# An attention and Fourier-mix kernel on one core: more weight decoding and hidden-layer work placed around the second batch's folds

## The chip, the cores and the metric

The kernel runs on one core of a Trainium2 chip. The core has a matrix engine (TensorE, in the profile PE, its weight loads PEld), a vector engine (VectorE, DVE), an activation engine (ScalarE, ACT), a general engine (GpSimd, POOL) and a queue that mostly starts transfers (SyncE, SP). Each engine takes its instructions in the order in which they stand in its program, and waits at an instruction until what that needs is there. The metric is the device time of one execution in microseconds (us).

## The reference

Everything is float32, except that the two weight matrices arrive as 64-bit floats. Four batches of 768 rows go through two blocks. First, causal attention with decay in 8 heads of width 64 (`lam` has one decay per head; it is written as a recurrence over blocks of 64 rows with a state of 64 x 64):

```
kv_state = lam_block * kv_state + (kb * rev_pow)^T vb
out      = ((qb kb^T) * Dmask) vb + (qb * lam_pow) kv_state
```

Its output, heads side by side, is a matrix x of 768 x 512 per batch. Then a Fourier mix and a two-layer network:

```
u   = x + real(fft(fft(x, axis=rows), axis=columns))
un  = (u - mean(u)) / sqrt(var(u) + 1e-6)          # each row
out = u + max(un @ w_ch1, 0) @ w_ch2               # 512 -> 2048 -> 512
```

## The kernel before, in words

**Attention** (`attn`, made of `attn_in` and `attn_out`) takes a batch in 6 chunks of 128 rows and the heads in 4 pairs. `attn_in` loads k, q and v (SP), transposes k and q on TensorE (L274, L279) and copies them (ScalarE L276, L281; VectorE L285 for the decayed q). `attn_out` makes scores (L298), multiplies them with the decay (VectorE L302), updates the state (L315, L320) and makes the transposed output (L328, L332), which ScalarE copies to `oT` (L335). `back` turns that into rows again: a transpose on TensorE (L348) and two copies by ScalarE (L350, L351), the second half of the columns reversed.

**The Fourier mix** (`fft_ln`) needs each row beside its mirror image, row 768 - s, to add and subtract the two ("fold"), which quarters the matrix products. The batches get the mirrored rows in two ways:

- The first batch (it is in `TURNED`) keeps a second, reversed copy of the transposed output, `oTs` (ScalarE L386; L392 in the last chunk), and transposes that too (`mirrored`).
- The others write their rows to DRAM from ScalarE's queue (L358, L360, L362) and read them back in mirrored order with indirect transfers of POOL (`mirror_a`, L431 and L437; `mirror_b`, L444).

VectorE then folds in several steps, `fold_a` over rows and `fold_b` over the rest (`fold_x` L418 to L422; L462 to L476). TensorE does the transform over rows (L508), ScalarE copies it (L512), and for three row tiles in turn TensorE does the one over columns (`width`, L521 to L526); VectorE puts the results together and adds x (L588 to L592, row 384 apart in L598 to L601). `norm` computes statistics (L538, L539, and L542, L543 on POOL), normalises (L556), and transposes on TensorE with a copy by ScalarE (L561, L562), or for groups that are used late writes the transposed rows to DRAM (L570) and u itself (L576).

**The weights** are decoded from 64-bit floats in 32 chunks (`load_weights`). A chunk is one transfer of 512 KB (SP, L209), two ScalarE instructions (L216, a sign; L218) and five on VectorE (L217, L220, L222, L224, L225). The raw chunk uses the same 4 buffers (`hp`) as the hidden layer. The order of the chunks is first half of `w_ch1`, first half of `w_ch2`, then the two second halves; the first 16 are what the first half of the hidden layer needs.

**The network** (`mlp`) takes 2 row tiles (a group) at a time, 12 groups in all. The first four (`PLAIN`) are computed directly: hidden blocks of 128 (L625, 4 products each), rectified in turn by ScalarE and VectorE (`fc % 2`; L633, L631) from a PSUM pool of 3 tiles, then the second product (L639), whose sum is added to u (L646, L647 for a first half; L650, L651 and a store for the rest). Three of the four are split into two halves of the hidden layer, `half[0]` and `half[1]`, so that work can start before all weights are decoded. The other eight groups (`late`) follow with fewer products (L712, L759), after VectorE has made sums of the weights (`combine_weights`, L689) and of their inputs (L702 to L705).

**The order of the work** is written by generators. Each yields an estimate of the time of what it has just issued, and `weave` and `beside` draw on two or more of them so that their estimates run in proportion: a larger yield lets the other generator issue more before the first goes on. A scheduler may then move instructions on an engine, except those pinned by `keep_in_program_order`. The lines around the change, L838 and L839:

```
run(beside(part(mix, T_FOLD), T_FOLD, att1, 2.5 * t_chunk))
run(beside(mix, 24.0, beside(att1, 3.5 * t_chunk, w, 0.12 * NW), 0.12 * NW + 2.5 * t_chunk))
```

Here `mix` is the first batch's Fourier mix, `att1` the second batch's attention, `w` the decoding, `NW` is 32. After that, the rest of the front (`fr`: second batch's last attention and its mix, then batches three and four) is woven with `half[0]` and the decoding, and later with `half[1]` and the fourth plain group. When the front is done, VectorE combines weights while TensorE finishes the plain groups; then comes `late`, from 440 us to the end.

Of the kernel before, what the change touches and what calls it, by code (L numbers as in the profile page):

```python
# [76 lines left out]
def kernel(  # L77
# [10 lines left out]
    nc = tc.nc  # L88
    B, H, S, D = q.shape
    DM = H * D  # L90
    DFF = moe_w_ch1.shape[1]
    C = 128
    NC = S // C
    HC = NC // 2
    HP = H // 2
    NK = S // 4 + 1
    KO = DM // 128
    FO = DFF // 128
# [3 lines left out]
    BLK = [128, S // 4 + 1 - 128]  # L102
# [12 lines left out]
    def front_pool(name, bufs):  # L115
        return front_end.enter_context(tc.tile_pool(name=name, bufs=bufs, side="left"))
# [8 lines left out]
    fp = front_pool("fp", 1)  # L125
# [13 lines left out]
    def new(pool, shape, tag, **kw):  # L139
        cnt[0] += 1  # L140
        return pool.tile(shape, F32, tag=tag, name=f"{tag}{cnt[0]}", **kw)
# [112 lines left out]
    ins, oTs, eo = {}, {}, {}  # L254
    LEADS = (0,)
    TURNED = (0,)
    first = const.tile([128, HP, 1], F32, name="first")
# [31 lines left out]
    def attn_out(b, c, head):  # L289
        kT, qT, qs, kd, vt = ins.pop((b, c))  # L290
        last = c == NC - 1


        mm = nc.tensor.matmul
        pss = [psum_a([C, HP, C]) for _ in range(2)]
        for hp in range(HP):
            for hi in range(2):
                mm(pss[hi][:, hp, :], lhsT=kT[HD[hi], hp, :], rhs=qT[HD[hi], hp, :], start=True, stop=True)  # L298
        sc = []
        for hi in range(2):  # L300
            t = new(at, [C, HP, C], "sc", bufs=3)
            nc.vector.tensor_tensor(t, pss[hi], decay[:, hi::2, :], op=ALU.mult)  # L302
            sc.append(t)
        if last and b - 1 in LEADS:
            mirror_a(b, pin=True)
        yield 1.5


        s_old, s_new = st[(c + 1) % 2], st[c % 2]
        if not last:  # L310
            pu = psum_a([128, HP, D])
            for hp in range(HP):
                for hi in range(2):
                    h = 2 * hp + hi
                    mm(pu[HD[hi], hp, :], lhsT=kd[:, h, :], rhs=vt[:, h, :], start=True, stop=True)  # L315
            if c == 0:
                nc.vector.tensor_copy(s_new, pu)
            else:
                nc.gpsimd.tensor_tensor(s_new, s_old, spow.broadcast_to([128, HP, D]), op=ALU.mult)
                nc.vector.tensor_tensor(s_new, s_new, pu, op=ALU.add)  # L320
            yield 0.9


        po = psum_a([128, HP, C])
        if c > 0:
            for hp in range(HP):
                for hi in range(2):
                    mm(po[HD[hi], hp, :], lhsT=s_old[HD[hi], hp, :], rhs=qs[HD[hi], hp, :],  # L328
                       start=(hp == 0), stop=False, skip_group_check=True)
        for hp in range(HP):  # L330
            for hi in range(2):
                mm(po[HD[hi], hp, :], lhsT=vt[:, 2 * hp + hi, :], rhs=sc[hi][:, hp, :],  # L332
                   start=(c == 0 and hp == 0), stop=(hp == HP - 1), skip_group_check=True)
        oT = new(at, [128, HP, C], "oT")
        nc.scalar.copy(oT, po)  # L335
        if b in TURNED:

            if c == 0:
                nc.scalar.copy(first, po[:, :, 0:1])
            elif c > 1:  # L340
                nc.scalar.copy(oTs[b][:, :, 0:1], po[:, :, 0:1])
        yield 2.0
        yield from head

        def back(oT, x, n=128):
            px = psum_a([C, HP, 128])
            for hp in range(HP):
                nc.tensor.transpose(px[:, hp, :], oT[:, hp, :], ident)  # L348
            px = px.rearrange("p h e -> p (h e)")
            nc.scalar.copy(x[0:n, 0:HM], px[0:n, 0:HM])  # L350
            nc.scalar.copy(x[0:n, HM:DM], px[0:n, DM - 1:HM - 1:-1])  # L351

        if b not in TURNED:
            x = xn_[b, c] = new(xp, [C, DM], "x") if c < HC else new(xn, [C, DM], "xn")
            back(oT, x)
            if c == 0:
                xd[b] = (dram.tile([S - 256, DM], F32, name=f"xa{b}"), dram.tile([257, DM], F32, name=f"xb{b}"))
                nc.scalar.dma_start(xd[b][1][256:257], x[0:1])  # L358
            elif not last:
                nc.scalar.dma_start(xd[b][0][(c - 1) * C:c * C], x)  # L360
            if c >= NC - 2:
                nc.scalar.dma_start(xd[b][1][(c - NC + 2) * C:(c - NC + 3) * C], x)  # L362
            if c == NC - 2 and b - 1 not in LEADS:
                mirror_a(b)
            elif last:
                mirror_b(b)
            yield 1.7
            return


        if c == 2:
            eo[b] = new_eo()

        def mirrored(m):
            if m < HC:
                back(oTs[b], eo[b][HC - 1 - m][1][:, 1, 0:DM], BLK[HC - 1 - m])
            else:
                u = xs[b, HC + NC - 1 - m] = new(xp, [128, DM], "x")
                back(oTs[b], u)

        if c > 1:
            mirrored(c - 1)
            yield 1.4
        if c > 0:
            oTs[b] = new(fp, [128, DM + 4], "ds")[:, 0:DM].rearrange("p (h c) -> p h c", h=HP)
            nc.scalar.copy(oTs[b][:, :, C - 1:0:-1], po[:, :, 1:C])  # L386
        if not last:
            x = xn_[b, c] = new(xp, [C, DM], "x") if c < HC else new(xn, [C, DM], "xn")
            back(oT, x)
            yield 1.7  # L390
        else:
            nc.scalar.copy(oTs[b][:, :, 0:1], first)  # L392
            mirrored(c)
            for t in range(HC):
                xs[b, t] = xn_.pop((b, t))
            yield 1.4
# [86 lines left out]
    def fft_ln(b):  # L483
# [7 lines left out]
        if b in LEADS:  # L491
            yield from fold_a(b)
            yield from fold_b(b, sets)
            yield 2.0
        else:
            yield 1.0
            run(fold_a(b))
            yield 3.0
            run(fold_b(b, sets))
            yield 9.0  # L500


        for i in range(5):
            ps = psum_a([128, 2, NK])
            m = 128 if i < 4 else 1
# [72 lines left out]
        for t in (1, 2, 0):  # L578
# [7 lines left out]
            ds = new(fp, [128, 2 * (HM + 2)], "ds")  # L586
# [3 lines left out]
            u, v_ = xs[b, t], xs[b, HC + t]  # L590
# [27 lines left out]
    def mlp(b, g, f0=0, f1=FO):  # L618

        ut = uts[b, g]  # L620
        hr = []
        for fc in range(f0, f1):
            ps = psum_m([128, G * 128])
            for c in range(KO):
                nc.tensor.matmul(ps, lhsT=w1[:, c, 128 * fc:128 * fc + 128], rhs=ut[:, c, :],  # L625
                                 start=(c == 0), stop=(c == KO - 1))
            if fc % 4 == 0:
                hr.append(new(hp_, [128, 4, G * 128], "hr"))
            t = hr[-1][:, fc % 4, :]
            if fc % 2:  # L630
                nc.vector.tensor_scalar(t, ps, 0.0, None, op0=ALU.max)  # L631
            else:
                nc.scalar.activation(t, ps, AF.Relu)  # L633
            yield 1.7
        for i in range(G):
            T = TT[g][i]
            ps = psum_m([128, DM])
            for fc in range(f0, f1):
                nc.tensor.matmul(ps, lhsT=hr[(fc - f0) // 4][:, fc % 4, 128 * i:128 * i + 128], rhs=w2[:, fc, :],  # L639
                                 start=(fc == f0), stop=(fc == f1 - 1))  # L640
                if fc % 4 == 3 and fc < f1 - 1:
                    yield 3.4
            u = xs[b, T]
            tt = nc.vector.tensor_tensor
            if f1 < FO:
                tt(u[:, 0:HM], ps[:, 0:HM], u[:, 0:HM], op=ALU.add)  # L646
                tt(u[:, HM:DM], ps[:, DM - 1:HM - 1:-1], u[:, HM:DM], op=ALU.add)  # L647
            else:
                y = new(up, [128, DM], "y", bufs=1)
                tt(y[:, 0:HM], ps[:, 0:HM], u[:, 0:HM], op=ALU.add)  # L650
                tt(y[:, HM:DM], ps[:, HM:DM], u[:, DM - 1:HM - 1:-1], op=ALU.add)  # L651
                store(b, T, y)
            yield 3.4
# [156 lines left out]
    def run(gen):  # L810
        return sum(gen)
# [12 lines left out]
    NW = 2 * KO * DFF // WP  # L824
    w = weights()
    t_chunk = 7.3
# [3 lines left out]
    def beside(lead, t, other, t_other):  # L830
        return weave(lead, part(other, t_other), t_other / t)

    att1, mix = attn(1), fft_ln(0)
    att0 = attn(0)
    run(part(att0, 2.7))
    run(beside(att0, NC * t_chunk - 2.7, w, 0.25 * NW))

    run(beside(part(mix, T_FOLD), T_FOLD, att1, 2.5 * t_chunk))  # L838
    run(beside(mix, 24.0, beside(att1, 3.5 * t_chunk, w, 0.12 * NW), 0.12 * NW + 2.5 * t_chunk))  # L839

    half = [[mlp(b, g, h * FO // 2, (h + 1) * FO // 2) for b, g in PLAIN[:3]] for h in range(2)]
    fr = chain([att1, fft_ln(1)] + [front(b) for b in range(2, B)])
# [4 lines left out]
    back = chain(half[1] + [mlp(*PLAIN[3])])  # L847
# [47 lines left out]
```

## Time and profile before

| what | value |
|---|---|
| device time, 6 runs | 828.12, 832.36, 832.6, 832.81, 832.88, 833.83 us; median 832.7 |
| the profiled execution | 833.2 us, of it 831.1 us from the first to the last instruction (the span); granted TensorE clock 0.993 of full |
| busy share of the span | PE 96%, PEld 77%, DVE 53%, ACT 22%, POOL 10% |

An execution's profile records each instruction with its start, its duration and the semaphores that it waited for. A row such as `L631 DVE ... x32 | 13.2, 412 | 32.7 <-PE pm L625 32.6` says: line 631, on VectorE, 32 instructions, 13.2 us busy in all, 412 ns on average; before them VectorE stood 32.7 us, of which 32.6 ended when line 625 of TensorE had written tile `pm`. In a timeline row come the start (us), the duration (us), engine, line, operation, tiles and shapes, and in brackets how long the engine stood before it, and what ended that. An engine name with a q (ACTq) is its instruction queue, where it starts transfers.

TensorE's time that went neither into its records nor their usual spacing lies in the front: PE is busy 55.58 of 62 us from 50 to 112 us, 13.90 of 18 from 112 to 130, 29.24 of 30 from 130 to 160, all of 160 to 260, 56.52 of 60 from 260 to 320, 89.94 of 92 from 320 to 412, and all of 412 to 440. VectorE is busy 52.08 of 62 from 50 to 112, and 25.01 of 28 from 412 to 440.

### The profile page before, as it was taken

The numbers are of one execution on the slowest core, as the hardware profiler recorded it, in microseconds if no ns is written. First come the engines' busy times: TensorE is split into PE (matmuls) and PEld (weight loads), VectorE is DVE, ScalarE is ACT, GpSimd is POOL, SyncE is SP. The second block draws the span as 40 slices with busy tenths as digits, with TensorE's granted clock in tenths as the row PEclk, the third lists the DMA queues.
The fourth block names the chain that finished last, engine by engine and source line by source line (L and its number), as shares of the span: only waits on it lengthen the run. The fifth ranks groups of instructions, "written<-read, shape, count | busy, mean of one in ns | idle before, by whom it ended". The sixth has DMA issues, their size and how long they took to land.

```text
span 831.1 us, 11682 instructions
## 1 busy us (share of the span) xinstructions
PE 799.7 (96%) x4608; PEld 636.4 (77%) x4608; DVE 443.5 (53%) x1030; ACT 183.0 (22%) x436; POOL 79.3 (10%) x102
## 2 busy tenths in 40 slices
PE   6989889999999999999999999999999999999998
PEld 5767765758675857767748888888888888888886
DVE  6889788857943582345895551156312561145411
ACT  4745343125520210312101210022001220012100
POOL 3112140012010110220100000000000000000000
PEclk9999999999999999999999999999999999999999
DMA  9966632247951128430442011100111001100010
GB/s 261 249 141 179 159 115 80 84 122 184 234 153 39 51 55 161 111 120 18 114 108 95 1 51 51 51 1 0 52 51 51 0 1 35 36 32 1 1 39 25
DMA packets 126683, 68.87 MB, mean 83 GB/s; under 512 B 111150, under 2 KB 112174, under 8 KB 126630
## 3 DMA queue, kind: packets, MB, share of 16 engines
q1 hardware_dynamic: 121488, 55.67, 26.3%
q0 software_dynamic: 2112, 6.69, 2.5%
q10 hardware_dynamic: 3030, 5.78, 1.9%
q8 instruction: 36, 0.59, 0.3%
q14 instruction: 17, 0.14, 0.1%
HBM read 48.72 MB, written 19.40 MB: 82 GB/s over the span
## 4 chain that ended last, share of the span: by engine, by line
PE 79%; DVE 11%; issue 4%; DMA 3%; ACT 2%; POOL 1%; POOLq 0%; DVEq 0%; ACTq 0%
PE p L759 23%; PE p L712 23%; PE pm L639 10%; PE pm L625 7%; PE pa L508 3%; PE pa L332 3%; PE pa L298 3%; PE pa L328 2%; DMA x<-xb,ix 2%; PE pa L274 1%; PE pa L315 1%; PE pa L348 1%; DVE stt L538 1%; PE pa L279 1%; DMA xb<-xn 1%
## 5 line engine op out<-in xcount | busy, mean ns | idle before, releaser
L625 PE MATMUL pm<-ut,w 128*128 128x256 f32 x512 | 119.1, 382 | 0.2 <-DVE hr L631 0.2
L639 PE MATMUL pm<-w,hr 128*128 128x512 f32 x256 | 118.0, 605 | 1.3 <-DVE hr L631 1.3
L625 PEld LDWEIGHTS pm<-ut,w 128*128 128x128 f32 x512 | 94.3, 190 | 15.4 <-issue 3.1
L712 PE MATMUL p<-ur,w 128*128 128x256 f32 x384 | 93.8, 379 | 0.0
L639 PEld LDWEIGHTS pm<-w,hr 128*128 128x128 f32 x256 | 46.9, 191 | 51.0 <-issue 47.6
L712 PEld LDWEIGHTS p<-ur,w 128*128 128x128 f32 x384 | 73.0, 190 | 10.3 <-issue 0.5
L712 PE MATMUL p<-us,w1s 128*128 128x256 f32 x256 | 65.7, 379 | 0.0
L759 PE MATMUL p<-w,hs 128*128 128x256 f32 x256 | 58.0, 379 | 0.5 <-DVE y L780 0.5
L759 PE MATMUL p<-w2s,hs 128*128 128x256 f32 x256 | 57.9, 379 | 0.0
L759 PE MATMUL p<-w,ha 128*128 128x256 f32 x256 | 57.9, 379 | 0.0
L759 PEld LDWEIGHTS p<-w,hs 128*128 128x128 f32 x256 | 48.5, 190 | 7.5 <-DVE y L780 0.9
L759 PEld LDWEIGHTS p<-w2s,hs 128*128 128x128 f32 x256 | 48.6, 190 | 6.6
L712 PEld LDWEIGHTS p<-us,w1s 128*128 128x128 f32 x256 | 48.6, 190 | 6.6
L759 PEld LDWEIGHTS p<-w,ha 128*128 128x128 f32 x256 | 48.6, 190 | 6.6
L614 POOL DMA_INDIRECT out_dram<-y,ix x12 | 11.9, 988 | 408.5 <-DVE y L785 344.0
L739 ACT COPY ha<-p 128x256 f32<-128x256 f32 x32 | 11.9, 372 | 169.1 <-PE p L712 139.4
L750 DVE TENSOR_TENSOR ha<-p,ha 128x256 f32<-128x256 f32 x32 | 13.6, 424 | 44.9 <-ACT ha L749 44.9
L302 DVE TENSOR_TENSOR sc<-pa,decay 128x512 f32<-128x512 f32 x48 | 31.3, 681 | 11.6 <-PE pa L298 11.6
L332 PE MATMUL pa<-sc,v 128*64 128x128 f32 x384 | 31.5, 281 | 5.4 <-DVE sc L302 5.4
L298 PEld LDWEIGHTS pa<-qT,kT 64*128 64x128 f32 x384 | 26.4, 195 | 12.1 <-ACT qT L281 5.4
L332 PEld LDWEIGHTS pa<-sc,v 128*64 128x64 f32 x384 | 22.9, 137 | 14.2 <-DVE sc L302 9.2
L298 PE MATMUL pa<-qT,kT 64*128 64x128 f32 x384 | 31.2, 295 | 2.5 <-ACT qT L281 2.2
(144 smaller groups left out, 1135.5 us busy)
## 6 DMA issues: line engine op xcount, KB each, us to landing
raw<-in_moe_w_ch_dram SPq DMA_DIRECT2D x32, 512.0 KB, 4.8
k<-in_k_dram SPq DMA_DIRECT2D x24, 256.0 KB, 4.8
q<-in_q_dram SPq DMA_DIRECT2D x24, 256.0 KB, 5.2
v<-in_v_dram SPq DMA_DIRECT2D x24, 256.0 KB, 3.7
ud<-x SPq DMA_DIRECT2D x16, 256.0 KB, 2.3
utd<-e SPq DMA_DIRECT2D x64, 64.0 KB, 2.2
u<-ud SPq DMA_DIRECT2D x16, 256.0 KB, 2.7
ur<-utd SPq DMA_DIRECT2D x6, 512.0 KB, 4.4
```

Of the source, the lines that this page charges most:

```text
L298: mm(pss[hi][:, hp, :], lhsT=kT[HD[hi], hp, :], rhs=qT[HD[hi], hp, :], start=True, stop=True)
L302: nc.vector.tensor_tensor(t, pss[hi], decay[:, hi::2, :], op=ALU.mult)
L328: mm(po[HD[hi], hp, :], lhsT=s_old[HD[hi], hp, :], rhs=qs[HD[hi], hp, :], start=(hp == 0), stop=False, skip_group_check=True)
L332: mm(po[HD[hi], hp, :], lhsT=vt[:, 2 * hp + hi, :], rhs=sc[hi][:, hp, :], start=(c == 0 and hp == 0), stop=(hp == HP - 1), skip_group_chec ...
L508: mm = nc.tensor.matmul(ps[0:m, n, :], lhsT=piece(a, i, n), rhs=cs[0:rows, a, i in (2, 3), n, :], start=(a == 0), stop=(a == 1))
L614: nc.gpsimd.indirect_dma_start(out=out.rearrange("b s d -> (b s) d"), out_offset=row_of(2 + HC * (b + 1) + T - HC), in_=y[:, :], in_offset ...
L625: nc.tensor.matmul(ps, lhsT=w1[:, c, 128 * fc:128 * fc + 128], rhs=ut[:, c, :], start=(c == 0), stop=(c == KO - 1))
L639: nc.tensor.matmul(ps, lhsT=hr[(fc - f0) // 4][:, fc % 4, 128 * i:128 * i + 128], rhs=w2[:, fc, :], start=(fc == f0), stop=(fc == f1 - 1))
L712: nc.tensor.matmul(ps, lhsT=s2.A[a][:, kt, 128 * i:128 * i + 128], rhs=U[b][:, kt, :], start=(first and kt == 0), stop=(kt == 1), skip_gro ...
L739: nc.scalar.copy(a11, two(X))
L750: V.tensor_tensor(a22, two(Z), a22, op=ADD)
L759: nc.tensor.matmul(ps, lhsT=h[a][:, s, i, :], rhs=s2.B[b][:, i, :], start=(first and i == 0), stop=(i == HF - 1), skip_group_check=True)
```

## The change

Four edits, all to the placement of work; what is computed stays the same.

1. In the first batch's attention, `back` is split into its transposes (`turn`) and its copies (`put`). The transposes of the previous chunk's mirrored rows are issued first, then the copies that fill the next `oTs` (now pinned in program order), then the copies of the mirrored rows.
2. For the second batch (`b - 1 in LEADS`) `fft_ln` yields 6.0 instead of 3.0 after `fold_a`, and 12.0 instead of 9.0 after `fold_b`.
3. In `half[0]` (`f1 < FO`) ScalarE does all rectifications; elsewhere they go on taking turns.
4. Beside the first batch's mix and the second batch's attention, 0.16 of the 32 chunks of weights are drawn instead of 0.12.

The diff:

```diff
@@ attn_out
-        def back(oT, x, n=128):
+        def turn(oT):
             px = psum_a([C, HP, 128])
             for hp in range(HP):
                 nc.tensor.transpose(px[:, hp, :], oT[:, hp, :], ident)
-            px = px.rearrange("p h e -> p (h e)")
+            return px.rearrange("p h e -> p (h e)")
+
+        def put(px, x, n=128):
             nc.scalar.copy(x[0:n, 0:HM], px[0:n, 0:HM])
             nc.scalar.copy(x[0:n, HM:DM], px[0:n, DM - 1:HM - 1:-1])
+
+        def back(oT, x):
+            put(turn(oT), x)
...
-        def mirrored(m):
+        def mirrored(m, px):
             if m < HC:
-                back(oTs[b], eo[b][HC - 1 - m][1][:, 1, 0:DM], BLK[HC - 1 - m])
+                put(px, eo[b][HC - 1 - m][1][:, 1, 0:DM][0:BLK[HC - 1 - m]], BLK[HC - 1 - m])
             else:
                 u = xs[b, HC + NC - 1 - m] = new(xp, [128, DM], "x")
-                back(oTs[b], u)
-
+                put(px, u)
+
+        px = turn(oTs[b]) if c > 1 else None
+        if c > 0:
+
+            oTs[b] = new(fp, [128, DM + 4], "ds")[:, 0:DM].rearrange("p (h c) -> p h c", h=HP)
+            tc.keep_in_program_order(nc.scalar.copy(oTs[b][:, :, C - 1:0:-1], po[:, :, 1:C]))
+        if last:
+            tc.keep_in_program_order(nc.scalar.copy(oTs[b][:, :, 0:1], first))
         if c > 1:
-            mirrored(c - 1)
+            mirrored(c - 1, px)
             yield 1.4
-        if c > 0:
-            oTs[b] = new(fp, [128, DM + 4], "ds")[:, 0:DM].rearrange("p (h c) -> p h c", h=HP)
-            nc.scalar.copy(oTs[b][:, :, C - 1:0:-1], po[:, :, 1:C])
         if not last:
             x = xn_[b, c] = new(xp, [C, DM], "x") if c < HC else new(xn, [C, DM], "xn")
             back(oT, x)
             yield 1.7
         else:
-            nc.scalar.copy(oTs[b][:, :, 0:1], first)
-            mirrored(c)
+            mirrored(c, turn(oTs[b]))
             for t in range(HC):
                 xs[b, t] = xn_.pop((b, t))
             yield 1.4
@@ fft_ln
         else:
             yield 1.0
             run(fold_a(b))
-            yield 3.0
+            yield 6.0 if b - 1 in LEADS else 3.0
             run(fold_b(b, sets))
-            yield 9.0
+            yield 12.0 if b - 1 in LEADS else 9.0
@@ mlp
-            if fc % 2:
+            if fc % 2 and f1 == FO:
                 nc.vector.tensor_scalar(t, ps, 0.0, None, op0=ALU.max)
             else:
                 nc.scalar.activation(t, ps, AF.Relu)
@@ the order
-    run(beside(mix, 24.0, beside(att1, 3.5 * t_chunk, w, 0.12 * NW), 0.12 * NW + 2.5 * t_chunk))
+    run(beside(mix, 24.0, beside(att1, 3.5 * t_chunk, w, 0.16 * NW), 0.16 * NW + 2.5 * t_chunk))
```

## The prediction

> **What bounds the kernel now.** I read the engines' shares first, then the stretches, the waits, and the timeline round the longest wait.
>
> ```profile
> PE 799.7 (96%) x4608; PEld 636.4 (77%) x4608; DVE 443.5 (53%) x1030; ACT 183.0 (22%) x436; POOL 79.3 (10%) x102
> ```
>
> TensorE sets the time. Its 4608 records are the same work after the change, so only time in which it stands, or runs at a lower clock, can be won or lost. By stretches (columns: span; busy us of PE, PEld, DVE, ACT, POOL; granted clock; DMA share, GB/s):
>
> ```profile
> 60.00:80.00 20.00, 16.94 (x174) 13.70 (x170) 19.96 (x42) 9.17 (x19) 4.40 (x5) 1.00 0.78 217
> 120.00:130.00 10.00, 6.88 (x18) 3.36 (x17) 8.09 (x21) 0.48 (x3) 0.78 (x1) 0.84 0.16 52
> 130.00:140.00 10.00, 10.00 (x47) 6.83 (x46) 8.66 (x21) 4.40 (x9) 0.00 (x0) 0.99 0.40 110
> 200.00:260.00 60.00, 60.00 (x417) 42.35 (x416) 38.90 (x79) 23.47 (x47) 8.37 (x8) 1.00 0.64 164
> ```
>
> Up to about 110 us VectorE is the limit (19.96 of 20); from 160 TensorE is full, but for short holes at the later folds. The worst ten microseconds are 120 to 130: PE busy 6.88, clock 0.84. The timeline tells why:
>
> ```profile
> 111.52 0.27 DVE L601 TENSOR_TENSOR x<-pa,xn 1x128 f32<-1x128 f32 x1
> 112.50 0.33 ACTq L362 DMA_DIRECT2D xb<-xn  x1
> 115.48 4.04 POOL L444 DMA_INDIRECT x<-xb,ix  x1 [0.54 <-DMA xb<-xn]
> 121.91 0.69 DVE L418 TENSOR_TENSOR fe<-x,x 128x512 f32<-128x512 f32 x1 [3.02 <-DMA x<-xb,ix]
> 125.38 0.57 PE L508 MATMUL pa<-cs,fe 128*128 128x193 f32 x2 [3.12 <-DVE fe L467]
> ```
>
> The second batch's last attention rows are written to DRAM (112.50), gathered back mirrored (115.48, landing 6.41 later), folded by VectorE (121.91), and only then comes the first length transform, L508. VectorE waited 3.02 for the gather, TensorE 3.12 for VectorE. The two engines that rectify:
>
> ```profile
> L631 DVE TENSOR_SCALAR hr<-pm 128x256 f32<-128x256 f32 x32 | 13.2, 412 | 32.7 <-PE pm L625 32.6
> L633 ACT ACTIVATE hr<-pm 128x256 f32<-128x256 f32 x32 | 12.2, 383 | 72.2 <-PE pm L625 68.7 <-DMA ur<-utd 3.5
> ```
>
> Prices of TensorE work: 32 records of L625 took 7.07 us at 247.74, so a block of 8 (one column block) is 1.77; 32 of L639 took 13.90, so the 16 of a row tile are 6.95.
>
> **The change part by part.** Order below means the order in which the changed kernel's instructions stand on each engine.
>
> *Work behind the second batch's folds* (two yields, 3 more each, and rectification off VectorE). Before, the first L508 stands after the first hidden blocks and one L639. After, between L601 and that L508 stand L332 (1.0), three L625 blocks (5.3), the norm's transposes and the row transposes L348 (0.9 and 0.6), two more blocks (3.5) and both row tiles of L639 (13.9): 25.2 us. Against it runs the chain of the fold, and this gets longer: the row copies (L350) now stand on ScalarE behind both copies of a norm's transposes, so they wait for statistics (1.3), POOL (1.1), the two normalisations among fold steps (about 3) and transposes and copies (1.5): 7 after L601, where they stood at 0.03. Then copies 0.65, xb write 2.7, issue 0.3, gather 6.4: 17.1; then the 8.2 that L418 took to the second L467 (121.91 to 130.1): 25.3 to 25.6. TensorE thus waits about 0.5 instead of 3.12: gain 2.6. Bounds: 3.1 if the gather lands in its median 3.4; below nothing if it lands 5 later.
> With the hole goes the lower clock: 0.84 over 10 us is 1.6 us of clock; taken whole, bounds 0 and 1.6. The Trainium skill, page "TensorE: Matmul & The Clock Gate", section "Why this matters for your kernels", wants no idle gap above about 3 us; the 3.12 ahead of the 0.84 agrees. By it 0.5 us of waiting is harmless and 1.6 comes back; by a stricter reading of the row, nothing does.
>
> *Chunks of weights moved.* One chunk is one 512 KB load on SP, two ScalarE instructions (683, 720 ns) and five on VectorE (L217 450, L222 431, L220 440, L224 709, L225 764, in a row 0.34, 0.34, 0.34, 0.60, 0.60: 2.2 us). The order has five instead of four of them ahead of the first batch's second norm, and two and a half more between the second batch's folds. The latter, 5.4 us, lie in the time in which VectorE would wait for the gather. The former lies on the stage that VectorE bounds: cost up to 2.2. Against it VectorE idled 2.96 at 94 for qT, and the order now puts the width steps L588 ahead of that wait. I take 0.5 lost; bounds 2.2 lost and 1.0 won. The loads pass the ud stores on SP, which wait until the norm anyway (x row tiles freed for batch 2 are asked for some 15 us later); where that cover goes, it is a few us of attention.
>
> *Rectification by ScalarE.* Twelve instructions leave VectorE (0.34 each in a row, 4.0 us) and cost ScalarE 12 by 0.38 (4.6). ScalarE was busy 4.4 of 10 at 130 to 140 and 23.5 of 60 later. The gain is that a hidden block no longer waits behind a fold or a decode on VectorE: at 130 to 160 TensorE lost about 1.9 (28.1 us of work at the paces above in 30). I take 0.7; bounds 1.9, and a loss of 1 if ScalarE is held by a sign step waiting for its load (10.8 in nine waits, the longest 2.9; three hidden tiles in PSUM cover 5 us).
> Here a rule speaks against the change: the Trainium skill, page "ScalarE: Activation LUTs", section "Rules for kernel authors", says relu belongs to VectorE, up to about three times faster in bf16. The rows here have float32 from PSUM: 412 on VectorE, 383 on ScalarE. By the rule's factor the move would cost 12 by 255 ns, 3.1 us of engine time; by the rows it saves 0.03 each. No run here shows bf16.
>
> *First batch's mirrored rows.* TensorE waited 1.32 (50.51) for L392, which stood behind two copies and L386. After, L386 and L392 stand first: L392 can end 0.86 earlier. VectorE idled 0.77 (52.71) just for that chain, so 0.8 is won; bounds 0 and 0.8. In two earlier chunks L386 falls behind a decode step; five PSUM banks cover that.
>
> *The end of the front.* The yields use up six units of the second batch's share, so four more hidden blocks of the last plain group are done before the front ends, and 7.07 us less cover stands after it. Before, L522 ended at 404.9, TensorE went over to L712 at 439.99, and the second operand product, which needs L703, came 1.73 later; L703 ended 436.94: 4.8 us of slack. After, VectorE has two L631 less (0.7): 7.07 - 4.8 - 0.7 = 1.6 lost. Bounds: 0 and 4.
>
> Nothing for the other folds: at the third batch both wait for the mlp's output (L651) as before; at the fourth the first wait (0.92) goes, but the second grows as much, since the fold sets it.
>
> **Sum**, against the profiled execution (831.1 span, 833.2 us): -2.6 -1.6 +0.5 -0.7 -0.8 +1.6 = -3.6, so 829.6. The profiled execution stands 0.5 above the median of the runs, 832.7, so I forecast 829.1.
>
> **Rivals.** About 0.3% (2.5 us) is what a measurement of this kernel can tell from no change.
> A, *more is won*: decode fits into the 2.96 us hole and the end keeps its slack: 829.1 - 0.5 - 1.6 = 827.0. For it: VectorE's idle time before 112. Against: VectorE is full from 412 to 438.
> B, *the hole only moves*: the fold stays 3 us late, the clock falls again, the end costs 1.6: 832.7 - 0.7 - 0.8 + 0.5 + 1.6 = 833.3, no change. For it: the chain starts 7 us later than it did.
> C, *slower*: VectorE runs in order, and ahead of the fold now stands L217 of a chunk whose buffer comes free only about 8.5 after L601. Its load (median 4.8) lands near 13.5, in time for a gather at 17. If write, gather and loads crowd each other so that the fold ends 5 us later, TensorE waits 5.5, the clock falls: 833.3 - 3.1 + 5.5 = 835.7. It decides from about 4.4 us of delay. Against it: the DMA share at 120 to 130 is 0.16.
>
> **How the numbers follow.** Forecast 0.50, A 0.14, B 0.20, C 0.16. Faster holds forecast and A, 0.64; same B, 0.20; slower C, 0.16. The forecast's own range is 826 to 831. The range for 8 in 10 starts at 825.0: with the gains at their upper bounds (3.1, 1.6, 1.9, 0.8, and 1.0 from decode) and the end's 1.6 lost it is 832.7 - 6.8 = 825.9, and about 825 if part of that loss is spared too. It reaches over all of B and up to 835.0, where C begins with 4.4 us of delay (833.3 - 3.1 + 4.9 = 835.1), so that C alone is left out.
>
> **What would show it.** Right: no wait above 1.5 us of L508 for L467 in the second batch, clock 1.00 from 110 on, VectorE at work where it stood 3.02, and TensorE in L639 just ahead of L508. L712 would wait about 1.6 for L703 at the end of the front. Wrong: a new wait of L217 (a decode step ahead of the fold) for its load, L633 waits that hold L625, or L601 more than 2 us later.

## The result, and the profile after

The changed kernel takes 827.45 us (median; 824.87 to 832.5), the kernel before 832.25 us in the same comparison. The ratio is 0.9949, with a 95% interval of 0.9939 to 0.9959: faster by half a per cent, 4.2 us. The profiled execution took 827.11 us, its span is 825.3 instead of 831.1.

The engines' shares on the changed kernel's page:

```profile
PE 794.3 (96%) x4608; PEld 634.3 (77%) x4608; DVE 439.6 (53%) x1018; ACT 186.5 (23%) x448; POOL 76.4 (9%) x102
```

TensorE has the same 4608 records in a shorter span; the twelve rectifications have gone from VectorE's 1030 to ScalarE's 448. The changed kernel's busy times by stretches (columns as in the prediction), three of those shown there and one more:

```profile
60.00:80.00 20.00, 17.15 (x178) 14.19 (x180) 19.97 (x43) 9.56 (x20) 3.83 (x4) 1.00 0.79 220
120.00:130.00 10.00, 10.00 (x30) 5.51 (x29) 6.69 (x14) 3.76 (x7) 2.48 (x2) 1.00 0.73 235
130.00:140.00 10.00, 9.93 (x36) 6.06 (x35) 10.00 (x29) 1.47 (x4) 0.00 (x0) 1.00 0.18 56
430.00:440.00 10.00, 7.66 (x29) 6.21 (x28) 7.15 (x13) 1.49 (x4) 1.08 (x1) 0.83 0.91 291
```

The hole of 120 to 130 us is closed: TensorE is busy 10.00 instead of 6.88, at clock 1.00 instead of 0.84. A new one has opened at 430 to 440: 7.66 busy, clock 0.83. In the kernel before, that stretch reads:

```profile
430.00:440.00 10.00, 10.00 (x25) 4.50 (x24) 8.14 (x10) 0.00 (x0) 0.00 (x0) 1.00 0.80 241
```

The timeline of the changed kernel round the second batch's fold (start, duration, engine, line):

```profile
112.25 0.27 DVE L609 TENSOR_TENSOR x<-pa,xn 1x128 f32<-1x128 f32 x1
...
119.18 0.38 ACT L352 COPY xn<-pa 128x256 f32<-128x256 f32 x1
...
119.86 0.33 ACTq L367 DMA_DIRECT2D xb<-xn  x1
...
122.18 1.54 POOL L452 DMA_INDIRECT x<-xb,ix  x1 [6.53 <-DMA xb<-xn]
...
128.40 0.69 DVE L426 TENSOR_TENSOR fe<-x,x 128x512 f32<-128x512 f32 x1 [2.12 <-DMA x<-xb,ix]
```

and TensorE's part of that timeline:

```profile
132.69 3.60 PE L647 MATMUL pm<-w,hr 128*128 128x512 f32 x8
136.12 3.13 PE L516 MATMUL pa<-cs,fe 128*128 128x193 f32 x16
```

L609 is L601 of before, L352 L350, L426 L418, L516 L508, L647 L639. The chain is longer, as forecast: the row copies start 6.9 us after L609 (forecast: 7), the gather lets VectorE go on 16.1 after (17.1). VectorE still stands 2.12 for it, but TensorE has second products (L647) until the fold is done and goes into L516 with no wait listed.

To see where the rest went I take, for each stretch, its length less TensorE's records at their full spacing in a row (0.216 us for L625 and the late L712 and L759, 0.430 for L639, 0.164 for L508, 0.11 for transposes and L521 to L526, 0.07 for L298, 0.064 for L328 and L332, 0.04 for L315). This is the time that TensorE lost to waits and to a lower clock. "End" runs from the first L712 to the last record.

| lost, us | 0–50 | 50–160 | 160–320 | 320–first L712 | end | sum |
|---|---|---|---|---|---|---|
| before | 19.3 | 22.9 | 10.6 | 4.7 | 0.9 | 58.3 |
| changed | 19.3 | 19.1 | 5.8 | 3.6 | 4.8 | 52.6 |

So 3.8 us were won between 50 and 160, 4.9 from 160 to 320 (mostly the third batch), 1.1 in the fourth batch, and 4.0 were lost at the end: 5.7 of the 5.8 between the spans of these two executions, where the medians differ by less.

### The profile page after: what moved, and what is told of

It reads as the page before. It is cut to its first block, busy times and chain, and to the rows that moved or that the text cites. A ratio compares the mean times of both kernels' runs of the same rounds, so it can differ in the third digit from the quotient of the medians.

```text
span 825.3 us, 11708 instructions
## 1 busy us (share of the span) xinstructions
PE 794.3 (96%) x4608; PEld 634.3 (77%) x4608; DVE 439.6 (53%) x1018; ACT 186.5 (23%) x448; POOL 76.4 (9%) x102
## 4 chain that ended last, share of the span: by engine, by line
PE 77%; DVE 14%; DMA 4%; issue 2%; ACT 1%; POOL 1%; SPq 0%; DVEq 0%; POOLq 0%; ACTq 0%
PE p L767 23%; PE p L720 23%; PE pm L633 9%; PE pm L647 7%; PE pa L516 2%; PE pa L332 2%; PE pa L298 2%; DMA x<-xb,ix 2%; PE pa L328 1%; PE pa L274 1%; DVE sc L302 1%; PE pa L315 1%; PE pa L279 1%; DMA raw<-in_moe_w_ch_dram 1%; DVE stt L546 1%
## 5 line engine op out<-in xcount | busy, mean ns | idle before, releaser
L647 PE MATMUL pm<-w,hr 128*128 128x512 f32 x256 | 116.0, 598 | 0.0
L647 PEld LDWEIGHTS pm<-w,hr 128*128 128x128 f32 x256 | 46.6, 190 | 49.5 <-issue 48.0
L720 PEld LDWEIGHTS p<-ur,w 128*128 128x128 f32 x384 | 73.6, 192 | 10.6 <-issue 0.5
L332 PE MATMUL pa<-sc,v 128*64 128x128 f32 x384 | 31.1, 280 | 8.3 <-DVE sc L302 8.2
L302 DVE TENSOR_TENSOR sc<-pa,decay 128x512 f32<-128x512 f32 x48 | 31.3, 681 | 12.0 <-PE pa L298 12.0
L298 PEld LDWEIGHTS pa<-qT,kT 64*128 64x128 f32 x384 | 25.1, 193 | 12.7 <-ACT qT L281 5.8
L332 PEld LDWEIGHTS pa<-sc,v 128*64 128x64 f32 x384 | 22.7, 137 | 15.3 <-DVE sc L302 10.6
L298 PE MATMUL pa<-qT,kT 64*128 64x128 f32 x384 | 29.8, 292 | 3.4 <-ACT qT L281 3.1
```

Source lines behind the costliest of these rows:

```text
L720: nc.tensor.matmul(ps, lhsT=s2.A[a][:, kt, 128 * i:128 * i + 128], rhs=U[b][:, kt, :], start=(first and kt == 0), stop=(kt == 1), skip_gro ...
```

## The experiments

Each was run beside the kernel before; the ratio is against that. The tables of lost time come from one profiled execution each and carry about 2 us of chance (see the last section); the ratios decide.

### Each part alone

The yields alone:

```diff
-            yield 3.0
+            yield 6.0 if b - 1 in LEADS else 3.0
...
-            yield 9.0
+            yield 12.0 if b - 1 in LEADS else 9.0
```

> Only the two yields of the second batch are raised (6.0 and 12.0); the rest is as before. In the order 10 L639 products of 0.87 us (a pair of records) stand ahead of the second batch's first L508, against 1 before, and one more chunk of decoding between its folds. Theory H (the gain is the hole at the second fold and its lower clock; the loss is cover at the end of the front): the 3.1 us wait of L508 goes and 112 to 130 us loses about 5 us less; L712 then waits for L703 about as long as in the changed kernel (2.3, and a half clock of 3.4 us after it, 1.7): 832.3 - 5.5 + 4 = 831, ratio 0.998. Rival W (the earlier decoding of weights carries the gain, the yields only move work): 832.3, ratio 1.000, or slower by the loss at the end, 1.005.

The weights alone:

```diff
-    run(beside(mix, 24.0, beside(att1, 3.5 * t_chunk, w, 0.12 * NW), 0.12 * NW + 2.5 * t_chunk))
+    run(beside(mix, 24.0, beside(att1, 3.5 * t_chunk, w, 0.16 * NW), 0.16 * NW + 2.5 * t_chunk))
```

> Only the share of weights beside the first batch's mix is raised from 0.12 to 0.16. In the order 7 L639 products stand ahead of the second batch's first L508, against 1, and about two and a half more chunks of decoding between its folds. By the prediction's own sum this part alone costs 0.5 us (ratio 1.001), since the stage up to 112 us is bound by VectorE and the fold is late anyway. Theory W: it carries most of the gain, since 6 more products (5.2 us) fill the hole of 3.1 and the clock stays up, with only one hidden block less of cover at the end: 832.3 - 5 + 1 = 828, ratio 0.995.

ScalarE's rectifications alone:

```diff
-            if fc % 2:
+            if fc % 2 and f1 == FO:
```

> Only the rectifications of the first halves all go to ScalarE. By the prediction's sum: 0.7 us won between 130 and 160 us, ratio 0.999; the order ahead of the second fold is as before, so L508 still waits about 3 us for L467. Rival: the 3.9 us that the changed kernel wins between 260 and 320 us come from here (no hidden tile waiting for L631): 828.4, ratio 0.995.

The mirrored rows alone (the first part of the change, shortened here):

```diff
-        if c > 1:
-            mirrored(c - 1)
+        px = turn(oTs[b]) if c > 1 else None
...
+            tc.keep_in_program_order(nc.scalar.copy(oTs[b][:, :, C - 1:0:-1], po[:, :, 1:C]))
+        if last:
+            tc.keep_in_program_order(nc.scalar.copy(oTs[b][:, :, 0:1], first))
+        if c > 1:
+            mirrored(c - 1, px)
```

> Only the order of the first batch's mirrored copies is changed. By the prediction's sum: L348 waits 0.5 to 0.8 us for L392 instead of 1.3, VectorE's gap of 0.77 before the next L302 goes, 0.8 us won, ratio 0.999. Rival K (the lower clock around 52 us is what counts, as TensorE works at half speed for 3.4 us there): it goes with the wait, 0.8 + 1.7 = 2.5 us won, ratio 0.997.

| kernel | ratio, 95% interval | lost 50–160 | 160–320 | end |
|---|---|---|---|---|
| yields alone | 0.9962, 0.9943 to 0.9981 | 16.5 | 6.4 | 4.4 |
| weights alone | 1.0059, 1.0038 to 1.0080 | 29.4 | 10.9 | 0.7 |
| ScalarE alone | 0.9998, 0.9980 to 1.0017 | 22.9 | 10.6 | 1.0 |
| mirrored rows alone | 0.9977, 0.9961 to 0.9994 | 20.9 | 10.2 | 0.9 |

The yields carry most of the gain, as theory H has it, and theory W falls: the weights alone cost 4.9 us. ScalarE's part alone shows no gain: the 3.9 us of its rival fall, and the sum's 0.7 is too small to be told from none. The interval of the mirrored rows holds both the sum's 0.999 and rival K's 0.997 and does not decide between them. The product of the four ratios is 0.9996, but the change measures 0.9949, so the parts do not simply add up. Where the weights alone lose is seen in that kernel's timeline:

```profile
110.93 0.69 DVE L418 TENSOR_TENSOR fe<-fo,xn 128x512 f32<-128x512 f32 x1 [3.62 <-DMA fo<-xa,ix]
113.74 0.68 DVE L302 TENSOR_TENSOR sc<-pa,decay 128x512 f32<-128x512 f32 x1
...
114.48 0.69 PE L332 MATMUL pa<-sc,v 128*64 128x128 f32 x2 [4.53 <-DVE sc L302]
```

The first step of the second batch's `fold_a` (L418 on `fo` and `xn`) now stands on VectorE ahead of the last scores (L302) and of the first batch's last additions. VectorE stands 3.62 us for the gather, and L302, which has its input, waits behind it; TensorE's L332 waits 4.53 for that. Nor is the hole ahead of the second batch's L508 filled, as theory W has it: it only comes later, with a wait of 3.50 for L467 that ends at 138.61. In the kernel before, the first fold step stood behind L601 and did not wait:

```profile
111.81 0.65 DVE L418 TENSOR_TENSOR fe<-fo,xn 128x512 f32<-128x512 f32 x1
```

### The change with one part undone

Without the yields:

```diff
-            yield 6.0 if b - 1 in LEADS else 3.0
+            yield 3.0
...
-            yield 12.0 if b - 1 in LEADS else 9.0
+            yield 9.0
```

> The changed kernel with the second batch's yields back at 3.0 and 9.0 (mirrored copies, ScalarE and 0.16 of weights stay). Theory H (the work behind the folds is what pays for the decoding put there): without it the extra decoding costs as it does alone, about 4.9 us, less 1.9 for the mirrored copies: 832.3 + 4.9 - 1.9 = 835, ratio 1.004; L508 of the second batch waits about 3 us again, and L712 no longer waits for L703. Rival P (the parts just add up: the changed kernel less the 3.2 us that the yields give alone): 827.5 + 3.2 = 830.7, ratio 0.998.

Without the extra weights:

```diff
-    run(beside(mix, 24.0, beside(att1, 3.5 * t_chunk, w, 0.16 * NW), 0.16 * NW + 2.5 * t_chunk))
+    run(beside(mix, 24.0, beside(att1, 3.5 * t_chunk, w, 0.12 * NW), 0.12 * NW + 2.5 * t_chunk))
```

> The changed kernel with the share of weights back at 0.12. Rival P (the parts add up): 827.5 - 4.9 = 822.6, ratio 0.989. Theory H (behind the longer yields the extra decoding lies in time in which VectorE would wait for the gather, and costs only what it takes up to 112 us, 2 to 4 us; at the end of the front less cover takes part of that back): yields and mirrored copies alone give 832.3 - 3.2 - 1.9 = 827.2, ratio 0.994.

Without ScalarE's part:

```diff
-            if fc % 2 and f1 == FO:
+            if fc % 2:
```

> The changed kernel with the rectifications of the first halves taking turns again. ScalarE's part alone was worth 0.1 us: 827.5, ratio 0.995, with the same stages. Rival: in the company of the other parts it is worth more, since VectorE has decoding and folds to do while hidden blocks stand behind them; then 112 to 160 us loses 2 us more and the time is 829.5, ratio 0.997.

| kernel | ratio, 95% interval | lost 50–160 | 160–320 | end |
|---|---|---|---|---|
| no yields | 0.9983, 0.9962 to 1.0004 | 25.7 | 9.1 | 0.7 |
| no extra weights | 0.9947, 0.9919 to 0.9975 | 23.4 | 6.5 | 1.6 |
| no ScalarE part | 1.0040, 1.0024 to 1.0056 | 23.4 | 6.9 | 7.8 |

The yields are worth about the same in company (0.34%) as alone (0.38%). The extra weights are worth nothing in company, though they cost 0.6% alone. And ScalarE's part, worth nothing alone, is worth 0.9% in company: without it the kernel is slower than before the change. Of the expectations, P holds for the yields and H for the weights; both for ScalarE's part were far off. The timeline of the kernel without that part shows the cause again, larger (columns as above):

```profile
110.09 0.69 DVE L426 TENSOR_TENSOR fe<-fo,xn 128x512 f32<-128x512 f32 x1 [4.94 <-DMA fo<-xa,ix]
...
113.64 0.69 PE L332 MATMUL pa<-sc,v 128*64 128x128 f32 x2 [5.50 <-DVE sc L302]
```

In the changed kernel the same step stands at the same place among the scores, but VectorE comes to it 2.3 us later (at 107.44 instead of 105.15), since four more decode steps and two of the width step were placed ahead of it; so it waits less:

```profile
108.70 0.69 DVE L426 TENSOR_TENSOR fe<-fo,xn 128x512 f32<-128x512 f32 x1 [1.26 <-DMA fo<-xa,ix]
...
111.26 0.43 PE L332 MATMUL pa<-sc,v 128*64 128x128 f32 x2 [1.60 <-DVE sc L302]
```

It is the extra weights with which ScalarE's part interacts. In all six kernels of this record that have the extra weights and do not hold the fold back, its first step stands ahead of the last two L302 on VectorE; in the other seven without a hold it stands behind them and does not wait. In the two of the six where VectorE still rectifies in the first halves it waits 3.62 and 4.94 us, in the four where ScalarE does it waits 0.68 to 1.67.

### Order or work: the slower kernel with the fold held back

Is it the twelve rectifications, or only where the fold stands? The kernel without ScalarE's part was run with `fold_a` of the second batch kept behind the last scores on VectorE:

```diff
...
-            nc.vector.tensor_tensor(t, pss[hi], decay[:, hi::2, :], op=ALU.mult)
+            scored[b] = nc.vector.tensor_tensor(t, pss[hi], decay[:, hi::2, :], op=ALU.mult)
...
-            run(fold_a(b))
+            if b - 1 in LEADS:
+                with tc.issue_after(scored[b].ins):
+                    run(fold_a(b))
+            else:
+                run(fold_a(b))
```

> The slow kernel no_act (all edits but ScalarE's, ratio 1.004), with one thing more: the second batch's fold_a is kept behind the last scores of its attention (L302) on VectorE. Theory O (no_act is slow since VectorE arrives at the fold's first step, L418, 4.9 us before its gather lands, with L302 queued behind it, so that L332 waits 5.5 us): L418 stands behind both L302, L332 waits about 1.5 us as before, the half clock at 110 us (6.8 us long) goes, and 50 to 130 us loses 4 to 6 us less: 836.4 - 5 = 831, ratio 0.998, down to 0.995 with the clock. Rival E (no_act is slow since VectorE has twelve more rectifications to do beside folds and decoding, 4 us of work): the time stays at 1.004.

Measured: 0.9952 (0.9935 to 0.9968), against 1.0040. In this kernel's timeline the same two instructions read:

```profile
110.79 0.43 PE L332 MATMUL pa<-sc,v 128*64 128x128 f32 x2 [0.60 <-DVE sc L302]
...
113.26 0.65 DVE L426 TENSOR_TENSOR fe<-fo,xn 128x512 f32<-128x512 f32 x1
```

The fold no longer waits, L332 waits 0.60 instead of 5.50, and with VectorE doing half of the rectifications the kernel is as fast as the changed one; its lost times (18.8 at 50 to 160, 5.8 at 160 to 320, 5.2 at the end) are the changed kernel's. Theory O holds and rival E falls: ScalarE's part did its work by when VectorE comes to the fold, not by the time of the rectifications (of which only one stands ahead of that step in the slow kernel).

Not all of the 7.9 us between the two spans lie at the fold, however. 4.6 are won between 50 and 160 us, which fits the 4.9 that L332 waits less; 1.1 come from 160 to 320, and 2.6 from the end, where the longest wait differs too. First without the hold, then with it (L724 is L712 of before, L659 L651, L715 L703):

```profile
PE p L720 <- DVE y L659: 5.2, 1, 5.2
...
PE p L724 <- DVE us L715: 2.3, 1, 2.3
```

Why holding the fold at 110 us changes the last wait of the front was not tried. The fold as the cause is shown for the part up to 160 us.

### The end of the front

The input sums of the first late step (L702 to L705, made into a function `input_sums`) ahead of the last weight sums, the rest as changed:

```diff
...
+    sums[0] = input_sums(0)
     run(combine_weights(1))
```

> The changed kernel with the first late step's input sums (L702 to L705) issued ahead of the last four weight sums (4.6 us of L689) instead of behind them. If the loss at the end of the front is the wait of L712 for L703 and the half clock that follows it, 2.3 + 1.7 go: 823.5, ratio 0.990. Rival: another wait takes its place (the weight sums, 4.6 us later, or the PSUM of the last row tile, L651, which the kernel with the yields alone waits 3.5 us for): 826 to 827.5, ratio 0.993 to 0.995.

Measured: 0.9936 (0.9914 to 0.9958), not told apart from 0.9949. The end loses 2.3 instead of 4.8: the wait for L703 is gone, and 1.3 us for a copy by ScalarE came in its place. In the profile that is 2.5 of the 4 us hoped for; the ratios do not show it.

Then the cover itself: the six units of yields counted in the front's total, so that the groups behind it are drawn more slowly.

```diff
-    t_rest, t_back = 3 * t_front - 5 * t_chunk, len(PLAIN) * t_mlp - 45.0
+    t_rest, t_back = 3 * t_front - 5 * t_chunk + 6.0, len(PLAIN) * t_mlp - 45.0
```

> The changed kernel, with the six added units of yields counted in the front's total (t_rest + 6.0), so that the groups behind it are drawn more slowly: 40 us of work instead of 28 stand behind the last width step if counted in products (34.7 in the kernel before). If the loss at the end is the lost cover, L712 starts without a wait and the stretch from L712 to the end loses 0.9 instead of 4.8: 827.5 - 4 = 823.5, ratio 0.990. Rival: the hidden blocks that stay behind are missed at the third and fourth batch's folds, which lose 2 to 4 us more between 260 and 412 us: 826 to 828, ratio 0.993 to 0.995.

(The cover is 33.0 us in this kernel by the order of its products, not 40; 27.8 in the changed one.) Measured: 0.9992 (0.9976 to 1.0008). The end loses 0.7, as the first theory has it; but 160 to 320 us loses 10.4 again instead of 5.8, and 50 to 160 us 23.6. The stretch of 260 to 320 us in the kernel before:

```profile
260.00:320.00 60.00, 56.52 (x320) 37.56 (x319) 36.12 (x86) 9.81 (x28) 8.17 (x12) 1.00 0.25 61
```

the same stretch in the changed kernel:

```profile
260.00:320.00 60.00, 58.95 (x345) 42.31 (x344) 35.63 (x85) 10.71 (x30) 7.05 (x11) 1.00 0.31 75
```

and in the one with the total raised:

```profile
260.00:320.00 60.00, 57.66 (x323) 38.43 (x322) 35.91 (x89) 9.49 (x28) 8.15 (x12) 1.00 0.24 59
```

TensorE is busy 56.52, 58.95 and 57.66 us: about half of what the third batch had won is given back. In the same stretch the three kernels have 64, 96 and 64 records of L625, so the changed kernel has four hidden blocks more there than the kernel before, and its end has four fewer. The rival named the right cause, but neither place nor size: from 260 to 412 us 1.7 more are lost than in the changed kernel, about 2 from 160 to 260, and 4.5 from 50 to 160. Theory and rival leave out these 4.5; half the clock at 69.99 and 114.36, where the changed kernel has all of it, goes with them. So what the changed kernel loses at the end it wins before 320 us, by the same hidden blocks. All seven kernels that have the long yields with the old total lose 5.8 to 6.9 at 160 to 320 and 1.6 to 7.8 at the end; all others lose 9.1 to 10.9 and 0.7 to 1.0.

### In search of a better version

Yields and mirrored rows, without the other two parts, once with the total raised and once with the sums first (to both, the edits shown above that undo the other two parts):

```diff
-    t_rest, t_back = 3 * t_front - 5 * t_chunk, len(PLAIN) * t_mlp - 45.0
+    t_rest, t_back = 3 * t_front - 5 * t_chunk + 6.0, len(PLAIN) * t_mlp - 45.0
```

> Yields and mirrored copies alone (ScalarE's part and the extra weights undone), with the six units counted in the front's total; 34.7 us of cover behind the last width step, as before, and 15 L639 products ahead of the second batch's first L508. By the runs so far: the front loses 45.6 us as with the yields alone, less 0 to 2 for the mirrored copies, and the end 0.9: in all 45 to 46.5 instead of 58.3, so 832.5 - 12 = 820.5, ratio 0.986; if the rest between the folds costs something, 0.990. Rival (the extra weights are needed to fill VectorE's wait for the gather): it is no faster than the changed kernel, 0.995.

```diff
...
+    sums[0] = input_sums(0)
     run(combine_weights(1))
```

> Yields and mirrored copies alone, with the first late step's input sums ahead of the last weight sums (as in the kernel with that order alone). With the fold behind the scores from the start and none of the extra decoding up to 112 us, the front should lose 44 to 46 us (45.6 with the yields alone), and the end about 2.3: 47.5 against 58.3, so 832.4 - 10.8 = 821.6, ratio 0.987, if the mirrored copies keep their 1.9 us beside the yields; 0.990 if they don't. Rival: what the yields win varies from execution to execution with the second fold's gather and the half clocks, and no combination stays clearly below 0.994: then the single changes do not add up.

Measured: 0.9942 (0.9921 to 0.9963) and 0.9937 (0.9914 to 0.9961). Neither reached what its expectation added up, and neither can be told from the changed kernel. The first loses about 10.5 us from 160 to 320, where the yields alone lose 6.4: the raised total takes that gain away here too. In the second, the end loses about 7 us instead of 2.3. L712 waited 3.4 us for the last plain group's output (L651), as in the kernel with the yields alone: each version of the end has its own last wait, since VectorE has all of that work to do before the late part can run (in the changed kernel it works from 411.8 to 436.5 without a break). Both results are those that the rivals named; the reasons that the rivals give for them were not tried.

## Why the prediction was right, and where not

The forecast was 829.1 against a median of 832.7 (3.6 us won); measured were 4.2. Step by step:

- **The hole and its clock** (-2.6 and -1.6). Right in mechanism, and near in size: from 112 to 130 us 0.7 are lost instead of 6.3, 5.6 won where the two terms make 4.2. TensorE came to L516 23.9 us after L609 (25.2 forecast), and VectorE's second L475 ended 24.4 after it (25.3 to 25.6). The yields alone give 0.9962. Two of the signs named did not come out: VectorE still stood for the gather, 2.12 instead of 3.02, and the clock fell once more, at 434 us.
- **Chunks of weights moved** (+0.5). This step failed. I priced a decode step by its 2.2 us on VectorE and took the fold as staying where it was. I had read the order for the decode steps, not for the first step of `fold_a`, which moved ahead of the last scores. The term depends on how long VectorE stands there: 1.26 us in the changed kernel, 3.62 with the weights alone, 4.94 without ScalarE's part. The whole part costs 4.9 us alone, more than twice its upper bound of 2.2; beside the other parts it costs nothing that can be measured (0.9947 without it). In the changed kernel, 100 to 112 us loses 3.7 instead of 1.3.
- **Rectification by ScalarE** (-0.7). Wrong reason. 130 to 160 us loses 1.9 in both kernels, and alone the part gives 0.9998. What it does is the order above: it is worth 7.6 us (1.0040 less 0.9949) beside the other parts, and with the fold held the kernel does as well without it (0.9952). The rows stay near each other (382 ns on ScalarE, 420 on VectorE in the changed kernel), so the Trainium skill's rule for relu ("ScalarE: Activation LUTs", section "Rules for kernel authors") finds no support here for float32 from PSUM; no run shows bf16.
- **Mirrored rows** (-0.8). The wait of L348 for L392 went from 1.3 to 0.8; alone the part gives 0.9977, 1.9 us with an interval of 0.5 to 3.2. The size fits; the profiles do not settle it, since the kernel with the yields alone also loses some 2 us less between 50 and 112 us, with the order there as before.
- **The end of the front** (+1.6). The mechanism was right: L712 waits for VectorE's L703 (L711 in the new numbering). The size was off: 4.0, its upper bound. The wait was 2.34 instead of 1.6, and half the clock followed for 3.4 us, which I had left out. From the chain of TensorE's waits:

```profile
PE p L720 <- DVE us L711: 2.3, 1, 2.3
```

- **"Nothing for the other folds".** Wrong: 4.9 us were won at 160 to 320 us. The wait of L639 for L631 at 300 us (1.29) and one of L332 (0.72) went; the rest is not in listed waits. I had looked only at what sets the end of each fold, not at the four hidden blocks that the yields put there, the same that are missing at the end.

Against the profiles: up to 160 us I had 5.2 won and 3.8 were (the decoding, mostly), the end cost 2.4 more, and 160 us to the end of the front, which I had put at zero, won 6.0: 3.6 - 1.4 - 2.4 + 6.0 = 5.8, as between the two spans. The sum came out near for the main step's sake and, for the rest, by luck: these errors offset each other. Rival A named the right time (827.0) for the wrong reasons: the end did not keep its slack. Rivals B and C did not happen: the fold came in time. The wait of L217 for its load ahead of the fold, a sign of C, is there, but 1.12 us long; VectorE still had 2.12 to stand for the gather afterwards.

## What to carry to other kernels

A scheduler's order is part of a change: a part that is worth nothing alone can decide the sign in company, by when an engine comes to an instruction that waits, with ready work behind it. So look in the new order for every instruction that waits for a transfer and ask what stands behind it on its engine; holding that step back (1.0040 without the hold, 0.9952 with it) tells order from work. And work used as cover is counted once: what fills a hole early is missing where it stood before.

## What was not expected of the hardware

**The clock goes by a grid.** Where the fourteen profiles show a lower clock between 15 and 815 us (all but the one of the yields alone do), it is half the clock for 3.41 us or twice that, and within a profile these steps lie on one grid (51.66, 92.62 and 126.75 in the kernel before are 12 and 10 steps apart). I compared each lowered step with the share of the step before it that TensorE's records cover. Of 29 lowered steps, 27 follow a step covered by at most 57%, two follow another lowered one. Of 24 steps covered by 50% or less, 22 were followed by half the clock; from 50 to 57% both occur (5 and 8). No single long wait is needed: the kernel before dropped at 51.66 after a step in which the longest wait was 1.32 us. The Trainium skill ("TensorE: Matmul & The Clock Gate", section "Part 1: The HAM clock gate") gives the same window and says that it runs freely; that it takes an idle window to lower the clock, as its table has it, does not agree with these rows. The grid would also account for some of the scatter: the kernel with the yields alone, whose order is the same up to 100 us, shows none of the steps at 51.66 and 92.62, and loses 12.6 us from 50 to 112 instead of 14.7.

**An indirect transfer's issue varies.** POOL was busy 1.2 to 6.2 us with the first of the two gathers of the second batch (L444), the same instruction in every kernel. In the kernels with the extra weights it took 1.2 to 2.7, in those without 2.8 to 6.2. Why was not tried.
